# Retention into a Strassen-like feed-forward: layer-1 input sums on GpSimd, decays on the values

## The chip, the cores and the metric

The kernel runs on one core of one Trainium2 chip. Five engines of that core share the work, each with its own in-order queue of instructions: TensorE (PE in the profile, its weight loads as PEld), VectorE (DVE), ScalarE (ACT), GpSimd (POOL) and SyncE (SP), which here only issues DMAs. Engines wait for each other through semaphores; an instruction that waits holds up all that stands behind it on its own engine. The metric is the device time of one execution in microseconds, lower is better.

## The reference

All numbers are float32. The first part is a recurrent retention over 4 batches, 8 heads, 768 tokens and 64 features a head; the second is a feed-forward layer on the 3072 tokens that come out of it, with a gate that uses softplus and erf.

```python
gamma = 1.0 - 2.0 ** (-5.0 - np.arange(H))
for t in range(S):
    state = gamma * state + einsum('bhd,bhe->bhde', k[:, :, t], v[:, :, t])
    y[:, :, t] = scale * einsum('bhd,bhde->bhe', q[:, :, t], state)
x = y.transpose(0, 2, 1, 3).reshape(B * S, H * D)      # 3072 x 512
h = x @ w_in                                           # 512 -> 2048
sp = np.maximum(h, 0.0) + np.log1p(np.exp(-np.abs(h)))
out = (h * erf(sp)) @ w_out                            # 2048 -> 512
```

## The kernel before

**Retention by chunks.** The tokens are cut into 24 chunks of 128, numbered j; six of them make one batch. For a chunk the decays are folded into the inputs: a key is multiplied by its head's decay to the chunk's end, a query by the inverse, so that the scores are a plain product with a causal mask, and the state is a sum of products of scaled keys and values. Chunks 0 to 5 are scaled by `ret_scale` and transposed by TensorE. From chunk 6 on `prepared(j)` does it on VectorE alone, as a generator that its caller advances step by step: it scales the keys in token order (`KQ[j][:, 0]`, L579), which the state products read; it scales a second copy of the keys, `KB[j]`, and the queries, both loaded in 32x32 blocks (L588, twice); and it transposes those two by blocks (L592, twice). `sub_begin` and `sub_visit` then run the scores (L670), the state products `KQ` times `V` (L690, L814), the products of the masked scores with `V` (L793) and the products with the state (L778). The masked scores are written by `sub_mask` (L677).

**Loads.** `load(j)` issues 34 DMAs for a chunk from SyncE, in this order: the keys in token order (L208), 16 blocks of queries and 16 of keys (L190, 16 KB each), and last the values (`load_values`, L218). Each of these waits until the eighth DMA before it has landed. The calls are written into the order of the kernel by hand: chunks 6 and 7 are loaded during group 3, chunk j+3 after the visit of chunk j.

**Feed-forward.** The first 512 tokens (groups 0 to 3, each a quarter of the hidden features) are done with plain products, while weights are still converted and summed on VectorE (`sum_in`, L385). From group 4 (`G0`) on, 256 tokens take two groups, one for each half of the hidden features, and both layers use a scheme with 7 products in place of 8, the first layer nested so that 26 products of 128x128 tiles do. For these, `x_sums(g)` forms 18 sums or differences of 128x128 tiles of the layer's input, `xs`, before the first of the two groups (L969; the list is `X_SUMS`, in which a sum may use an earlier one). `xs` has one buffer, so its sums can only be written when the group before has read the old ones. `hidden_steps(g)` runs the 26 products in the order of `STEPS` (L987), each of which reads one sum or one input tile, and puts each into one of four PSUM banks, two named `hp` and two named `r`; it then adds the bank to the hidden blocks it belongs to (L999 on VectorE, L1001 and L1003 on ScalarE for the first of each block). The `r` banks are the ones that the scores use too.

**Order of a later group.** The 26 products, with parts of the second layer of the group before (`project_part`, L1070) between them; softplus on ScalarE (L859); the visit of a retention chunk; before an even group, `x_sums` of the next; on the others the preparation of a chunk; erf (L866); four more parts of the second layer; then the gate, two products on VectorE (`gated`, L885). In group 4 the order is written out apart: `prepared(6)`, `x_sums(4)`, the gate of group 3, the weight sums of the first half, the first step of `prepared(7)`, two weight sums, `sub_states(6)` (the mask and a state copy, L703), and then the 26 products.

**GpSimd** has almost no work: constants, small products of decay scales with 8 elements a partition (L496) or 32 (L522), and eight accumulating DMAs of 512 KB that form sums of the second layer's weights (`sums`, L394), each behind a negation on ScalarE (L393); the last of them stand in group 5.

Of the kernel before, what the change touches and what calls it, by code (L numbers as in the profile page):

```python
# [19 lines left out]
ALU = mybir.AluOpType  # L20
PSUM = bass.MemoryType.PSUM

P = 128
# [58 lines left out]
X_SUMS = (  # L82
    (0, (1, 0), (1, 1), "-"),
    (1, (0, 0), (0, 1), "-"),
    (2, (0, 0), (1, 0), "-"),
    (3, (1, 1), (0, 1), "-"),
    (4, (3, 0), (2, 0), "-"),
    (5, 1, 2, "-"),
    (6, (2, 0), 1, "+"),
    (7, (3, 1), 0, "-"),  # L90
# [39 lines left out]
)  # L130

OP = {"+": ALU.add, "-": ALU.subtract}

# [4 lines left out]
def kernel(  # L140
# [13 lines left out]
    nc = tc.nc  # L154
    B, H, S, D = q.shape
    d_model, d_ff = w_in.shape
    HP = H // 2
    NC = S // C
# [21 lines left out]
    KQ, V, KB = {}, {}, {}  # L180
# [39 lines left out]
    kq_s = const.tile([P, NC, 2, H], F32, name="kq_s")  # L220
# [268 lines left out]
    by = const.tile([P, H], F32, name="by")  # L489
# [13 lines left out]
    kq_b = const.tile([P, NC, 2, HP, 4], F32, name="kq_b")  # L503
# [71 lines left out]
    def prepared(j):  # L575

        if j >= NJ:
            return
        nc.vector.tensor_tensor(  # L579
            KQ[j][:, 0], KQ[j][:, 0],  # L580
            kq_s[:, j % NC, 0, :, None].to_broadcast([P, H, D]), op=ALU.mult,
        )
        yield
        blocks = (KB[j], KQ[j][:, 1].rearrange("p h d -> p (h d)"))
        for i, x in enumerate(blocks):
            x = x.rearrange("p (u a d) -> p u a d", u=HP, d=32)
            by = kq_b[:, j % NC, i, :, :, None].to_broadcast([P, HP, 4, 32])
            nc.vector.tensor_tensor(x, x, by, op=ALU.mult)  # L588
            yield
        for name, store, x in zip("kq", (KT, QT), blocks):  # L590
            store[j] = ret.tile([P, HP, C], F32, name=name + "T")
            nc.vector.transpose(store[j].rearrange("p u t -> p (u t)"), x)  # L592
            yield
# [354 lines left out]
    G0 = n_ft // FG  # L948
# [5 lines left out]
    def chunk_of(g):  # L954
        return TCH // SCH + (g - G0) // 2

    def x_sums(g):

        m = chunk_of(g)
        xs = ret.tile([P, N_X, P], F32, name="xs", bufs=1)  # L960

        def of(x):
            if isinstance(x, int):
                return xs[:, x]
            at = m % 2 * SCH + x[1] * P
            return XC[m // 2][:, x[0], at : at + P]

        for to, a, b, sign in X_SUMS:
            nc.vector.tensor_tensor(of(to), of(a), of(b), op=OP[sign])  # L969
        XS[m] = of  # L970

    def h_block(g, o):
# [251 lines left out]
    j = JPC + 2  # L1224
    sum_in(0, 20)
    all_of(prepared(j))
    x_sums(G0)
    load(j + 2)
    gated(G0 - 1)
# [3 lines left out]
    put_first(0)  # L1233
    sum_in(0, len(W_SUMS))
    next_chunk = prepared(j + 1)
    next(next_chunk)
    sum_in(1, 2)
# [28 lines left out]
    for g in range(G0 + 1, NG):  # L1266
# [4 lines left out]
        e_sums = g_sums(g - 1)  # L1271
        next(e_sums)
        next_chunk = prepared(j + 1) if even or put is None else iter(())

        if put is not None:
# [25 lines left out]
        if g + 1 < NG and not even:  # L1301
            x_sums(g + 1)
# [16 lines left out]
    g, m = NG - 1, chunk_of(NG - 1)  # L1319
# [10 lines left out]
    for i in range(2):  # L1330
# [4 lines left out]
        else:  # L1335
            last = ps_h.tile([P, TCH], F32, name="hp")[:, :P]
            a, b = PRODUCTS[3]
# [50 lines left out]
```

## Time and profile before

| | us |
|---|---|
| median of two runs | 661.3 |
| the two runs | 660.94, 661.66 |
| span of the profiled execution | 659.9 |
| a run's time beyond that span | 1.0 to 1.8 |
| TensorE busy | 654.1 |
| VectorE busy | 504.4 |
| ScalarE busy | 289.6 |
| GpSimd busy | 21.5 |

The profiled execution has no time of its own beside its span: what lies around the span is taken as the difference to the two runs, 1.4 us in the middle. The span is the time from the first to the last instruction. Busy times are sums over an engine's instructions; where an engine is busy for the whole of a stretch, only less work on it or a higher rate shortens that stretch. TensorE's ends are modelled, so its starts are the safer reading.

### The profile page before, as it was taken

The page shows a single profiled execution, that of the slowest core. Times are in us where ns is not written, and L with a number is a line of the kernel's source. Part 1 is how long each engine was busy: PE and PEld are TensorE (multiplying, and loading weights), DVE is VectorE, ACT ScalarE, POOL GpSimd, SP SyncE. Part 2 cuts the span into 40 slices and gives each one's busy share as a digit, 9 for nine tenths or more (in the row PEclk, how much of TensorE's full clock was granted, in tenths as well). Part 3 has the DMA queues.
Part 4 walks back from the last instruction along what each step waited for, and adds up shares of the span by engine and source line. Part 5 has one row for each costly group of instructions (what it writes and reads, how often), then busy time and mean ns, then how long its engine had stood idle before and what let it go on. Part 6 is the DMA issues. An engine that isn't in the chain of part 4 may idle for free.

```text
span 659.9 us, 15375 instructions
## 1 busy us (share of the span) xinstructions
PE 654.1 (99%) x6240; PEld 556.8 (84%) x6240; DVE 504.4 (76%) x1112; ACT 289.6 (44%) x410; POOL 21.5 (3%) x49
## 2 busy tenths in 40 slices
PE   8999999999999999999999999999999999999998
PEld 7744444487999999999999999999999999999997
DVE  5999879988886886787778678677787788476464
ACT  3468584527625334244254253342432542543440
POOL 1000061101100000000000000000000000000000
PEclk9999999999999999999999999999999999999999
DMA  9999972555843321222222322222231210000000
GB/s 190 222 236 220 211 246 43 107 100 120 165 77 59 79 47 35 68 44 48 68 46 45 73 39 50 60 52 42 38 80 34 45 55 1 1 35 1 1 32 33
DMA packets 157511, 51.90 MB, mean 79 GB/s; under 512 B 141312, under 2 KB 147840, under 8 KB 157440
## 3 DMA queue, kind: packets, MB, share of 16 engines
q1 hardware_dynamic: 155328, 46.71, 33.3%
q0 software_dynamic: 1696, 4.21, 3.4%
q8 instruction: 49, 0.80, 0.5%
q14 instruction: 22, 0.18, 0.1%
q10 hardware_dynamic: 416, 0.01, 0.0%
HBM read 40.39 MB, written 6.29 MB: 71 GB/s over the span
## 4 chain that ended last, share of the span: by engine, by line
PE 95%; DVE 3%; DMA 1%; SPq 0%; issue 0%; ACT 0%
PE o L1070 37%; PE hp L987 23%; PE r L987 12%; PE hp L896 8%; PE o L932 6%; PE r L778 2%; PE hp L670 1%; PE o L814 1%; DMA kq<-in_k_dram 1%; DVE w_in_sb L385 1%; PE r L599 1%; PE o L646 1%; PE r L793 1%; DVE xs L969 1%; PE hp L793 1%; PE r L566 1%
## 5 line engine op out<-in xcount | busy, mean ns | idle before, releaser
L987 PE MATMUL hp<-xs,w_in_sb 128*128 128x128 f32 x1040 | 145.6, 275 | 0.0
L1070 PE MATMUL o<-w_out_sb,h 128*128 128x256 f32 (+1 forms) x640 | 142.7, 380 | 0.0
L987 PEld LDWEIGHTS hp<-xs,w_in_sb 128*128 128x128 f32 x1040 | 135.2, 192 | 4.0 <-issue 0.7
L999 DVE TENSOR_TENSOR h<-h,hp 128x256 f32<-128x256 f32 x200 | 82.1, 419 | 73.6 <-PE hp L987 68.5
L1070 PEld LDWEIGHTS o<-w_out_sb,h 128*128 128x128 f32 x640 | 119.5, 190 | 16.6
L1070 PE MATMUL o<-w_out_sb,e 128*128 128x256 f32 x480 | 113.5, 379 | 0.0
L859 ACT ACTIVATE e<-h 128x2048 f32<-128x2048 f32 x22 | 42.0, 1910 | 120.6 <-DVE h L999 120.6
L1070 PEld LDWEIGHTS o<-w_out_sb,e 128*128 128x128 f32 x480 | 86.8, 190 | 9.4
L999 DVE TENSOR_TENSOR h<-h,r 128x256 f32<-128x256 f32 x160 | 59.9, 416 | 21.7 <-PE r L987 20.6
L1001 ACT COPY h<-hp 128x256 f32<-128x256 f32 x40 | 14.9, 373 | 134.6 <-PE hp L987 106.5
L987 PE MATMUL r<-xs,w_in_sb 128*128 128x128 f32 x480 | 66.7, 275 | 0.4 <-DVE am L677 0.4
L987 PEld LDWEIGHTS r<-xs,w_in_sb 128*128 128x128 f32 x480 | 60.0, 192 | 0.6 <-PE hp L987 0.6
L896 PE MATMUL hp<-xT,w_in_sb 128*128 128x512 f32 (+2 forms) x144 | 56.6, 548 | 0.0
L885 DVE TENSOR_TENSOR e<-h,e 128x1024 f32<-128x1024 f32 x42 | 49.3, 1213 | 8.0 <-ACT e L866 8.0
L987 PE MATMUL hp<-xT,w_in_sb 128*128 128x128 f32 x320 | 48.9, 275 | 0.0
L896 PEld LDWEIGHTS hp<-xT,w_in_sb 128*128 128x128 f32 x144 | 25.7, 190 | 27.2 <-issue 24.6
L987 PEld LDWEIGHTS hp<-xT,w_in_sb 128*128 128x128 f32 x320 | 43.6, 192 | 1.5 <-issue 0.5
L866 ACT ACTIVATE e<-e 128x2048 f32<-128x2048 f32 (+1 forms) x23 | 42.1, 1836 | 0.2
L1003 ACT ACTIVATE h<-hp 128x256 f32<-128x256 f32 x60 | 23.0, 384 | 31.1 <-PE hp L987 29.8
L987 PE MATMUL r<-xT,w_in_sb 128*128 128x128 f32 x240 | 33.3, 275 | 0.0
L866 ACT ACT_TABLE_LOAD x24 | 30.8, 1283 | 0.4
L987 PEld LDWEIGHTS r<-xT,w_in_sb 128*128 128x128 f32 x240 | 30.0, 192 | 0.0
(176 smaller groups left out, 778.6 us busy)
## 6 DMA issues: line engine op xcount, KB each, us to landing
w_out_sb<-in_moe_w_out_dram SPq DMA_DIRECT2D x14, 512.0 KB, 7.8
kq<-in_k_dram SPq DMA_DIRECT2D x23, 256.0 KB, 4.0
v<-in_v_dram SPq DMA_DIRECT2D x23, 256.0 KB, 3.4
out_dram<-r SPq DMA_DIRECT2D x23, 256.0 KB, 2.7
kq<-in_q_dram SPq DMA_DIRECT2D x288, 16.0 KB, 1.8
kb<-in_k_dram SPq DMA_DIRECT2D x288, 16.0 KB, 1.7
w_in_sb<-in_moe_w_in_dram SPq DMA_DIRECT2D x8, 512.0 KB, 13.2
w_out_sb<-w_out_sb POOLq DMA_DIRECT2D x8, 512.0 KB, 5.1
```

The costliest lines, as they stand in the source:

```text
L778: nc.tensor.matmul(pp[r][col * D : (col + 1) * D, u % 2, t], x[own, u, :], QT[j][own, u, t], start=first(r, col), stop=True, skip_group_ch ...
L793: nc.tensor.matmul(other[a][own, u % 2, D:] if crossed else pp[a][own, u % 2, t], V[j][t, 2 * u + r, :], AM[j][t, r, u, :D], start=crossed ...
L859: nc.scalar.activation(E[g], HS[g], AF.Softplus)
L866: nc.scalar.activation(E[g][:, half], E[g][:, half], AF.Erf)
L885: nc.vector.tensor_tensor(E[g][:, half], HS[g][:, half], E[g][:, half], op=ALU.mult)
L896: nc.tensor.matmul(HP_[ft][:, t], w_in_of(ft, kk), XC[0][:, kk, t], start=(kk == 0), stop=(kk == n_k - 1),)
L932: nc.tensor.matmul(O[0][tt].rearrange("p (d c) -> p d c", d=2), E[g][:, u * TCH + tt * P : u * TCH + (tt + 1) * P], w_out_of(ft), start=(f ...
L987: nc.tensor.matmul(to[:, u, :], w_in_sb[:, s, w, u * P : (u + 1) * P], XS[m](x), start=first and u == 0, stop=True, skip_group_check=True,)
L999: nc.vector.tensor_tensor(h, h, of, op=ALU.add if plus else ALU.subtract)
L1001: nc.scalar.copy(h, of)
L1003: nc.scalar.activation(h, of, AF.Copy, scale=-1.0)
L1070: nc.tensor.matmul(O[m][i][:, half, at], G[g][a][:, u * P : (u + 1) * P], w_out_sb[:, s, OUT[b], u, at], start=i not in started, stop=(s = ...
```

## The change

Two edits. In `prepared(j)`, from chunk 6 on, the values `V[j]` are multiplied by the decays of the keys, in place of the keys in both their copies; the queries are scaled as before. A score row weighted with scaled values, and the products for the state, come out the same, since each term holds one key and one value. Of the three products per chunk two remain; the place of the dropped one is kept as an empty step, so that the steps of the generator stand where they stood. In `x_sums` the 18 sums run on GpSimd for all but the first of the ten calls, and in all ten they follow a new order, `X_ORDER`; which sums there are, and of what, stays.

```diff
+X_ORDER = (1, 2, 5, 6, 9, 12, 13, 14, 0, 7, 15, 8, 4, 10, 11, 16, 17, 3)
 ...
         nc.vector.tensor_tensor(
-            KQ[j][:, 0], KQ[j][:, 0],
-            kq_s[:, j % NC, 0, :, None].to_broadcast([P, H, D]), op=ALU.mult,
+            V[j], V[j], kq_s[:, j % NC, 0, :, None].to_broadcast([P, H, D]), op=ALU.mult,
         )
         yield
+        yield
         blocks = (KB[j], KQ[j][:, 1].rearrange("p h d -> p (h d)"))
-        for i, x in enumerate(blocks):
-            x = x.rearrange("p (u a d) -> p u a d", u=HP, d=32)
-            by = kq_b[:, j % NC, i, :, :, None].to_broadcast([P, HP, 4, 32])
-            nc.vector.tensor_tensor(x, x, by, op=ALU.mult)
-            yield
+        x = blocks[1].rearrange("p (u a d) -> p u a d", u=HP, d=32)
+        by = kq_b[:, j % NC, 1, :, :, None].to_broadcast([P, HP, 4, 32])
+        nc.vector.tensor_tensor(x, x, by, op=ALU.mult)
+        yield
 ...
-        for to, a, b, sign in X_SUMS:
-            nc.vector.tensor_tensor(of(to), of(a), of(b), op=OP[sign])
+        engine = nc.vector if g == G0 else nc.gpsimd
+        for n in X_ORDER:
+            to, a, b, sign = X_SUMS[n]
+            engine.tensor_tensor(of(to), of(a), of(b), op=OP[sign])
```

## The prediction

> **What bounds the kernel now.** I read the page's busy times first, then the stages by group, then the timeline around the lines that change.
>
> ```profile
> PE 654.1 (99%) x6240; PEld 556.8 (84%) x6240; DVE 504.4 (76%) x1112; ACT 289.6 (44%) x410; POOL 21.5 (3%) x49
> ```
>
> ```profile
> 133.00:159.00 26.00, 25.59 (x238) 19.36 (x237) 22.83 (x59) 13.56 (x24) 1.74 (x2) 1.00 0.56 112
> 211.00:237.00 26.00, 26.00 (x291) 24.37 (x290) 20.00 (x52) 10.15 (x17) 0.00 (x0) 1.00 0.28 62
> ```
>
> The second view has two stages (length, then busy PE, PEld, DVE, ACT, POOL, then the granted clock). In a later group TensorE is busy for all of it at clock 1.00, and its products follow each other without a gap (eight 128x128 ones in 0.89 us, all along the chain). VectorE has some 6 us in 26 to spare. So work taken off VectorE shortens nothing by itself in groups 5 to 23, while a TensorE wait of any length moves the end by that length: no stretch behind it has idle time to take it back. The whole gain open to any such change is TensorE's idle time, 659.9 − 654.1 = 5.8 us. Faster by 2% (13.2 us), about what a measurement of this kernel can tell from no change, is all but excluded. The question is which waits are added. The matrix products are the same in number and order.
>
> **Part 1: values scaled in place of keys.** Eighteen chunks lose one 128x512 product of 0.68 us on VectorE. Nearly all of that time is idle cover in a bound TensorE stage: gain 0. The exception could be group 4:
>
> ```profile
> 131.32 0.69 PE L670 MATMUL r<-qT,kT 64*64 64x64 f32 x32
> ...
> 131.81 0.69 DVE L579 TENSOR_TENSOR kq<-kq,kq_s 128x512 f32<-128x512 f32 x1
> ...
> 132.53 0.47 SPq L218 DMA_DIRECT2D v<-in_v_dram  x1
> ...
> 133.08 0.75 DVE L677 TENSOR_TENSOR am<-r,causal_d 128x256 f32<-128x256 f32 x2
> ...
> 133.97 0.35 PE L987 MATMUL r<-xs,w_in_sb 128*128 128x128 f32 x1 [0.41 <-DVE am L677]
> ```
>
> The product at 131.81 is the first step of chunk 7's preparation. TensorE is late here: its third product of group 4 needs an `r` bank that the mask and the state copy on VectorE still read, and waits 0.4 us (against its usual distance, 133.39 to 133.97, 0.58). The dropped product of chunk 6 stood just ahead (its first step at 118.56), so VectorE would come 0.6 us earlier and this stall would go: −0.6 us if nothing else were late.
>
> But what is scaled now is the value tile, and it is the last of the chunk's 34 loads. The keys of chunk 7 were issued at 113.98; its values at 132.53, and they need 3.56 us:
>
> ```profile
> L218 SPq DMA_DIRECT2D v<-in_v_dram x1: 473/473/473, 132.5 to 132.5; - x1
> ...
> DMA to landing us min/median/max: 3.6/3.6/3.6
> ```
>
> So they land at 136.1, while VectorE asks for them at 131.8, or 131.2 with the dropped product. SyncE's pace in this stretch is set by landings of the small block loads (16 in 8.2 us, 16 in 9.7 us), which the change leaves alone. VectorE therefore stands still until 136.1, and behind the waiting product are two weight sums, the two masks and the state copy, which free the `r` bank. All of it slips by 136.1 − 131.8 = 4.3 us, and TensorE's product goes from 133.97 to 138.3. Behind that TensorE is bound to the end: **+4.3 us**, with the 0.6 us swallowed. Bounds: −0.6 if the values were there in time; +5.4 if they took 4.7 us, the slowest landing of the value loads behind them.
>
> For the other chunks I held each L218 landing (issue plus its landing time) against the L579 start: chunk 6 116.9 against 118.6, chunk 8 156.2 against 162.0, later ones 7 to 18 us early, with one close one, chunk 10 (203.56 against 203.70), in a group where VectorE has 2.5 us of idle time before the next product needs it. Cost there 0.
>
> **Part 2: sums on GpSimd.** Nine calls of 18 sums, 162 in all. On VectorE a sum starts every 0.20 us (0.28 long). Before, they end 1.5 us ahead of the first product that reads one. GpSimd's price is not in the trace, so I build it from its two-input rows:
>
> ```profile
> 5.33 0.21 POOL L496 TENSOR_TENSOR kq_s<-kq_s,by 128x8 f32<-128x8 f32 x1 [2.76 <-DVE kq_s L493]
> 5.63 0.73 DVE L556 TENSOR_TENSOR kq<-kq,kq_s 128x512 f32<-128x512 f32 x1
> 5.90 0.53 POOL L496 TENSOR_TENSOR kq_s<-kq_s,by 128x8 f32<-128x8 f32 x1
> ...
> 112.29 0.46 DVE L385 TENSOR_TENSOR w_in_sb<-w_in_sb 128x256 f32<-128x256 f32 x1
> 112.55 0.30 POOL L522 TENSOR_TENSOR kq_b<-kq_b,by_b 128x32 f32<-128x32 f32 x1
> ```
>
> Free, 8 elements take 0.21 us. Beside a VectorE product of two SBUF tensors the same takes 0.53 and ends 0.07 us after that product's end; with 32 elements, 0.10 after, and so do all five of that row. So the two engines exclude each other in such instructions, and what is left behind the lock grows by some 1.7 ns an element (0.04 us over 24). A free 128-element sum is then 0.21 + 120 × 1.7 ns = 0.41 us; one that waits for the sum before it starts 0.08 later (0.28 from start to start at 8 elements). Lower bound 0.29 (a one-input 128x128 selection, L459); upper 0.66, if the whole step from 0.21 to 0.30 over 24 elements is the rate. I take 0.41: a sum reads plain rows as the 8-element row does, the 32-element one reads a broadcast.
>
> By the Trainium skill's GPSIMD Engine Reference, section 3.1, a two-input add of 2048 elements takes 4497 ns; a line from the 8-element row to that gives an estimate of 0.46 us, and with it the sum below would be 0.4 us higher. No run here shows it yet.
>
> Now the race in a later group, with the profile's times:
>
> ```profile
> 229.08 0.56 DVE L834 TENSOR_TENSOR xT<-xT,hp 128x128 f32<-128x128 f32 x2 [0.44 <-ACT xT L832]
> ...
> 230.64 1.91 ACT L866 ACTIVATE e<-e 128x2048 f32<-128x2048 f32 x1
> ...
> 235.46 0.61 PE L987 MATMUL hp<-xs,w_in_sb 128*128 128x128 f32 x4
> ...
> 235.91 0.61 PE L987 MATMUL r<-xs,w_in_sb 128*128 128x128 f32 x4
> ```
>
> GpSimd can start at 229.45, 0.09 after the first of the two additions that complete the input. Seven sums, four of them waiting, are done by 232.56. The gate's two products (1.22 us each, two SBUF inputs) come when erf ends at 232.55, earlier than before since VectorE no longer has the sums; each holds GpSimd, with one sum between. The eighth sum (needed at 235.91) is done by 234.13, the ninth (236.35) by 235.6, the tenth (236.80) by 236.1, the fifteenth (239.48) by 238.3. Smallest margin 0.7 us: cost 0 in eight of nine calls. The same walk with 0.50 us a sum uses the margin up; with 0.66 the fifteenth comes 2.5 us late in every call.
>
> The first call, in group 5, differs: on GpSimd's queue stands the last accumulating DMA, which waits for its negation.
>
> ```profile
> 178.46 0.87 POOL L394 DMA_DIRECT2D w_out_sb<-w_out_sb  x1 [6.50 <-ACT w_out_sb L393]
> ```
>
> The sums start at 179.33, not 177.3. The gate comes at 181.5 after five sums, so the eighth is done at 184.99, while its product stands at 184.06: **+1.0 us** (0 without the lock, 4.2 at 0.66).
>
> **Sum.** 659.9 + 4.3 + 1.0 = 665.2 of span, plus the 1.4 us around it: **666.6 us**, 0.8% above the median of 661.3.
>
> **Rivals.**
> - *GpSimd too slow (slower).* From 0.50 us a sum on, each of the eight ordinary calls stalls TensorE; at 0.66 that is 8 × 2.5 + 4.2 + 4.3 = 28.5, so 690 us. For it: the 0.09 us step over 24 elements. Against: all 32-element products there ended behind a VectorE product, so that step is lock as much as rate. Over 2% needs about 1 us a call, some 0.57 us a sum. Chance 0.12; 0.05 more for small stalls (668 to 674).
> - *The value wait is not paid (no change).* If the values land before 131.2, the 0.6 us are won and only the first call costs: 661.7; without the lock 660.7. For it: the landings stand under two large accumulating DMAs whose timing may move. Against: the 5 us gap between issue order and need. Chance 0.11.
> - *The price falls elsewhere:* faster by over 2% would need work to leave TensorE; 0.01.
> - The forecast, 664 to 668.5: 0.71.
>
> By the Trainium skill's SBUF — State Buffer, section "Who interferes with whom", a VectorE instruction with only one SBUF input does not contend with GpSimd; the trace has no such pair. If the additions from PSUM (L999, from 237.5 on) contended too, the last needed sums would slip by 0.7 us, inside their 1.2 us of margin.
>
> Range 660.5 to 676: from the case without the value wait up to stalls of about 1.2 us in each ordinary call; it leaves out the slow end of the first rival. Faster 0.01, within 2% 0.87, slower 0.12.
>
> **What would show it.** After the change: VectorE idle some 4.5 us before the scaling of `v` at 131 to 136, released by a DMA of `in_v`; the first `r` product of group 4 waiting close to 5 us for `am`; GpSimd busy 70 to 90 us more, its sums 0.41 long when free and over 1 us under a gate; TensorE idle 1 us for `xs` in group 6 and not later. The prediction is wrong if group 4 runs as before, or if TensorE waits for GpSimd in every even group.

## The result and the profile after

The changed kernel takes **668.1 us** (668.08 to 668.11) against 661.3: a ratio of 1.0105, 95% interval 1.0088 to 1.0121. On the chip of a later experiment it took 668.3 against 661.1, ratio 1.0103 (1.0082 to 1.0125). The span of the profiled execution went from 659.9 to 666.4 us. The profiled execution of the kernel before is a rather long one of its kind: the median span of 29 later executions is 659.2, and of 21 others 659.4. One of the four executions of a later run, the one with the old order of the sums, took 845.5 us at a granted clock of 0.75 throughout and is left out. From the page after the change, busy time by engine:

```profile
PE 655.2 (98%) x6240; PEld 558.1 (84%) x6240; DVE 464.5 (70%) x932; ACT 289.9 (44%) x410; POOL 108.7 (16%) x211
```

VectorE lost 40 us of work, GpSimd took on 87, and TensorE, with the same 6240 products, sits idle for 11 us instead of 6. Line numbers are one to three higher than before in the places that matter. Two rows from the view of waits, for TensorE's products (total us, times, longest):

```profile
PE r L990 <- DVE am L678: 4.3, 1, 4.3
...
PE r L990 <- POOL xs L972: 0.9, 1, 0.9
```

From group 4 on these are the only two waits that are new in size: one for the mask in group 4, one for a sum on GpSimd. Both were forecast. The timeline of the first, start and length in us:

```profile
131.78 0.47 SPq L220 DMA_DIRECT2D v<-in_v_dram  x1
...
135.50 0.69 DVE L581 TENSOR_TENSOR v<-v,kq_s 128x512 f32<-128x512 f32 x1 [5.13 <-DMA v<-in_v_dram]
136.10 0.75 DVE L387 TENSOR_TENSOR w_in_sb<-w_in_sb 128x256 f32<-128x256 f32 x2
136.77 0.75 DVE L678 TENSOR_TENSOR am<-r,causal_d 128x256 f32<-128x256 f32 x2
...
137.67 1.66 PE L990 MATMUL r<-xs,w_in_sb 128*128 128x128 f32 x7 [4.34 <-DVE am L678]
```

Read it upwards: the third product waits for the masks, which stand behind two weight sums, which stand behind the scaling of the values, which waits 5.1 us for the last load of the chunk. The product starts at 137.67 instead of 133.97, 3.7 us later (3.9 when the 0.2 us that TensorE was ahead by then is counted).

The row counts seven instructions in 1.66 us. In the kernel before, eight at the same place took 1.13:

```profile
133.97 1.13 PE L987 MATMUL r<-xs,w_in_sb 128*128 128x128 f32 x8 [0.41 <-DVE am L677]
```

This is the part that the forecast did not have. The stretch in stages of 1 us; the columns are length, busy TensorE with its instructions, granted clock, DMA share and GB/s:

```profile
137.00:138.00 1.00, 0.33 (x2) 0.93 0.98 171
138.00:139.00 1.00, 1.00 (x7) 0.50 0.37 56
...
141.00:142.00 1.00, 1.00 (x10) 0.86 0.18 29
142.00:143.00 1.00, 1.00 (x11) 1.00 0.23 35
```

After the idle time TensorE's granted clock is halved for some 3.4 us (0.07 + 3 × 0.50 + 0.14 lost, doubled), and it does 6 or 7 instructions in a microsecond where it does 11 at full clock. It comes out 1.6 us further behind: 5.3 us in all when the clock is back. Of these, 0.2 come back at 143.7, where two products of the kernel before stood further apart. The wait in group 6 adds 1.0, and 0.2 more right behind it: the same 0.16 us stands there in all six profiled executions that have this wait, and in none of the four in which it is gone. Another 0.2 us of small delays was not followed up. 3.7 + 1.6 − 0.2 + 1.0 + 0.4 is the 6.5 us of the span.

### The profile page after: what moved, and what is told of

Its sections match the earlier page's. It is cut to its first block, busy times and chain, and to the rows that moved or that the text cites. A ratio compares the mean times of both kernels' runs of the same rounds, so it can differ in the third digit from the quotient of the medians.

```text
span 666.4 us, 15484 instructions
## 1 busy us (share of the span) xinstructions
PE 655.2 (98%) x6240; PEld 558.1 (84%) x6240; DVE 464.5 (70%) x932; ACT 289.9 (44%) x410; POOL 108.7 (16%) x211
## 4 chain that ended last, share of the span: by engine, by line
PE 89%; issue 7%; DMA 1%; POOL 1%; ACT 1%; DVE 0%; SPq 0%; POOLq 0%; ACTq 0%
PE o L1073 35%; PE hp L990 20%; PE r L990 11%; PE hp L897 8%; PE o L933 7%; PE r L779 1%; PE hp L671 1%; PE o L815 1%; POOL xs L972 1%; DMA kq<-in_k_dram 1%; DMA w_out_sb<-w_out_sb 1%; PE r L600 1%; PE o L647 1%; PE r L794 1%; PE r L568 1%
## 5 line engine op out<-in xcount | busy, mean ns | idle before, releaser
L990 PEld LDWEIGHTS hp<-xs,w_in_sb 128*128 128x128 f32 x1040 | 135.5, 192 | 3.9 <-issue 0.7
L972 POOL TENSOR_TENSOR xs<-xT 128x128 f32<-128x128 f32 x54 | 32.6, 623 | 331.7 <-DVE xT L835 331.7
L886 DVE TENSOR_TENSOR e<-h,e 128x1024 f32<-128x1024 f32 x42 | 52.8, 1297 | 35.4 <-ACT e L867 35.4
```

The source lines that it names most:

```text
L886: nc.vector.tensor_tensor(E[g][:, half], HS[g][:, half], E[g][:, half], op=ALU.mult)
L972: engine.tensor_tensor(of(to), of(a), of(b), op=OP[sign])
L990: nc.tensor.matmul(to[:, u, :], w_in_sb[:, s, w, u * P : (u + 1) * P], XS[m](x), start=first and u == 0, stop=True, skip_group_check=True,)
```

## The experiments

The explanation to test has three terms: the wait for the values (3.9 us net), the halved clock behind it (1.6 us), and the first call of the sums on GpSimd (1.0 us), with nothing for the other eight calls.

### One edit at a time

First the sums on GpSimd alone, with the keys scaled as before in `prepared`:

```diff
-            V[j], V[j], kq_s[:, j % NC, 0, :, None].to_broadcast([P, H, D]), op=ALU.mult,
+            KQ[j][:, 0], KQ[j][:, 0],
+            kq_s[:, j % NC, 0, :, None].to_broadcast([P, H, D]), op=ALU.mult,
...
+        for i, x in enumerate(blocks):        # KB[j] and the queries, as before
```

> The keys are scaled as before, in both copies; the sums stay on GpSimd in the new order. Theory: without a product that needs the values, the wait in group 4 goes, and with it the slow products behind it; only the first call of the sums still costs 1.0 us (and 0.3 us of small gaps): 662.3 to 662.6 us, GpSimd busy as in the changed kernel. Rival, the sums on GpSimd cost more than their one visible wait, by slowing VectorE's two-input products everywhere: 664 us or more.

Measured: 662.2 us against 660.9, ratio 1.0028 (1.0003 to 1.0053), 0.1 under the expected stretch. From group 4 on TensorE's only new wait is the one of 1.02 us from product to product in group 6, and the clock stays at 1.00 behind it. So the sums cost this one wait with the 0.2 us behind it, and their contention with VectorE costs nothing that shows. (The profiled execution took 666.0 us, since a weight load that landed late held up ScalarE, and with it TensorE, for 2.2 us at 87 us, with 3.4 us at half clock behind it; some executions of the kernel before reach 664 to 667 too.)

Then the scaled values alone:

```diff
-        engine = nc.vector if g == G0 else nc.gpsimd
+        engine = nc.vector
```

> The values are scaled as in the changed kernel; all ten calls of the sums run on VectorE, in the new order. Theory: the wait for the values (3.9 us more than the stall before) and the slow products behind it (1.6 us) stay, the 1.0 us in group 6 goes: 666.6 to 667.1 us. Rival, the sums on GpSimd share in the wait of group 4 (their DMAs or their lock): below 665.5 us.

Measured: 667.7 us, ratio 1.0086 (1.006 to 1.0112), 0.6 above the expected stretch. In its profiled execution the values landed later, at 136.6, the wait was 5.2 us, and the clock stayed at half for twice as long:

```profile
138.00:139.00 1.00, 0.21 (x1) 0.50 1.00 197
...
143.00:144.00 1.00, 1.00 (x6) 0.50 0.22 35
144.00:145.00 1.00, 1.00 (x8) 0.59 0.21 33
```

From 138.0 to 144.8 is 6.8 us, two of the earlier stretches. The halved clock is thus the term that varies: 1.6 us in one execution, 2.9 in another. The ten times of this kernel go from 666.5 to 669.5.

### The values first

```diff
         if j >= NB:
             KB[j] = loads.tile([P, HP * C], F32, name="kb", bufs=2)
-            nc.sync.dma_start(KQ[j][:, 0], k[b, :, now, :].rearrange("h p d -> p h d"))
+            load_values(j)
             load_blocks(KQ[j][:, 1].rearrange("p h d -> p (h d)"), q[b, :, now, :])
             load_blocks(KB[j], k[b, :, now, :])
...
+        if j >= NB:
+            nc.sync.dma_start(KQ[j][:, 0], k[b, :, now, :].rearrange("h p d -> p h d"))
-        if not early:
+        elif not early:
             load_values(j)
```

> From chunk 6 on the values are the first of a chunk's 34 loads and the keys in token order the last; all else as in the changed kernel. Theory: the values of chunk 7 land some 15 us before they are needed, TensorE's stall in group 4 falls from 4.5 us to 0 to 0.6 us, no product runs at half rate, the 1.0 us in group 6 stays: 661.3 to 662.3 us. Rival, VectorE is late there for another reason and the wait only changes its releaser: above 665 us.

Measured: 662.1 us against 660.9, ratio 1.0011 (0.9992 to 1.0031). The timeline around the place:

```profile
129.86 0.69 DVE L583 TENSOR_TENSOR v<-v,kq_s 128x512 f32<-128x512 f32 x1
...
132.52 0.76 DVE L680 TENSOR_TENSOR am<-r,causal_d 128x256 f32<-128x256 f32 x2 [1.31 <-PE r L693]
...
133.43 0.79 PE L992 MATMUL r<-xs,w_in_sb 128*128 128x128 f32 x5
```

The values are scaled at 129.9 without a wait; the mask is now the one that waits, for TensorE's state products (L693), and TensorE's third product follows at its usual distance, 0.55 us earlier than in the profiled execution of the kernel before. So the stall of that execution is gone too. The times do not show it as a gain: they lie 1.25 us above those of the kernel before, about as far as with the sums alone (1.3). Since its profiled execution was 0.7 us longer than its median, the stall may have been in that execution and not in most; there is no second trace of it. Two loads that swap places at the ends of the queue undo 6 us of the changed kernel's 668.1.

### Is it the idle time that halves the clock?

```diff
     for n, _ in enumerate(hidden_steps(G0), start=1):
+        if n == 2:
+            for _ in range(18):
+                nc.tensor.matmul(spare_bank, ident, ident, start=True, stop=True)
```

> The changed kernel, with 18 products of the identity with itself, some 4.0 us of TensorE work into a bank that nobody reads, put between the second and the third product of group 4, where TensorE waits for the values. Theory, the products behind the wait run at half rate because TensorE was idle: the wait stays, the granted clock is 1.00 all through, and the time falls by 1.6 us to 666.3 to 666.7. Rival, they run slow because of what they wait for (operands, banks) or the extra work costs what it saves: 668 us or more, products still 0.21 us apart.

Measured: 666.9 us, ratio 1.0089 (1.0055 to 1.0122); the expected 666.3 to 666.7 lies just below the median and well inside the spread of 666.1 to 667.8 that seven of the eight times have. The time alone decides little here. The trace does:

```profile
133.58 4.18 PE L1249 MATMUL o<-ident 128*128 128x128 f32 x36
136.75 0.69 DVE L581 TENSOR_TENSOR v<-v,kq_s 128x512 f32<-128x512 f32 x1 [4.91 <-DMA v<-in_v_dram]
138.93 1.13 PE L990 MATMUL r<-xs,w_in_sb 128*128 128x128 f32 x8 [1.17 <-DVE am L678]
```

```profile
140.00:141.00 1.00, 1.00 (x11) 1.00 0.14 23
```

(Each of the 18 products shows as two instructions.) VectorE waits 4.9 us for the values, which land 1.25 us later in this execution than in the changed kernel's, and the same third product starts late, at 138.93; but eight instructions behind it take 1.13 us and the clock is 1.00 throughout. Filled idle time, no slow products: the idle time is the cause, not what the products wait for.

### A shorter wait

```diff
-            load_blocks(KB[j], k[b, :, now, :])
+            load_blocks(KB[j], k[b, :, now, :], j)     # load_values(j) ahead of its last 4 blocks
```

> The changed kernel with a chunk's values issued 4 of its 16 key blocks sooner, so some 2.4 us. Theory: TensorE's stall in group 4 falls from 4.5 to about 2.1 us, which shows that the landing alone sets it. For the slow products behind it there are two cases: if any wait brings them in proportion, about 0.8 us of loss is left, 664.7; if only a wait of more than some length does, none is left and it comes to 663.9.

Measured once: 662.7 us. (In this and the other two runs that were measured once, the kernel before was also run once beside them and took 664.9, so that their times alone say little; the traces carry them.) The values were issued at 128.5 and landed at 131.9, 3.6 us earlier and not 2.4, so only 0.85 us of the stall is left and the case that I wanted, a wait of 2 us, did not come about. What it does show: 3.65 us less wait together with no slow product is 5.3 us, and the time fell by 5.4 from the changed kernel's 668.1.

### The first call of the sums

The group 6 race, in the changed kernel:

```profile
183.57 0.87 POOL L396 DMA_DIRECT2D w_out_sb<-w_out_sb  x1 [7.02 <-ACT w_out_sb L395]
184.14 1.20 POOL L972 TENSOR_TENSOR xs<-xT 128x128 f32<-128x128 f32 x2
...
186.53 1.37 DVE L886 TENSOR_TENSOR e<-h,e 128x1024 f32<-128x1024 f32 x1 [3.56 <-ACT e L867]
186.78 1.44 POOL L972 TENSOR_TENSOR xs<-xT,xs 128x128 f32<-128x128 f32 x1
...
188.29 1.31 POOL L972 TENSOR_TENSOR xs<-xT,xs 128x128 f32<-128x128 f32 x1
...
190.20 1.16 PE L990 MATMUL r<-xs,w_in_sb 128*128 128x128 f32 x8 [0.86 <-POOL xs L972]
```

Five sums, the gate, a sum stretched to 1.44, another to 1.31, and the eighth ends at 190.14, just ahead of the product that waited for it. The first two begin 0.57 us behind the start of the DMA and take 0.8 us each in place of 0.46, so that the third stands where it would if they had waited for the DMA's 0.87 us to end. The DMA ahead of them is the suspect for the late start:

```diff
+        if g + 1 < NG and not even:
+            x_sums(g + 1)
         if g == G0 + 1:
             all_of(last_steps)
-        if g + 1 < NG and not even:
-            x_sums(g + 1)
```

> The changed kernel with the last accumulating DMA behind the sums of group 6 on GpSimd's queue, not ahead of them. Theory: the sums start 0.1 us behind the chunk's last addition as in the other calls, and the wait of 1.0 us in group 6 is gone; the waits in group 4 stay: TensorE waits for no sum, about 667 us. Rival, the first call is late for another reason, such as a first use of the operation: the wait stays at 0.8 us or more.

Measured once: 667.9 us, and TensorE waits for no sum at all; the wait for `am` is unchanged at 4.3 us. The time fell by less than 1.0 only because the clock stayed at half for twice as long in this execution (2.9 us lost instead of 1.6). So the queue on GpSimd made the first call late.

### The order of the sums

```diff
-        for n in X_ORDER:
+        for n in range(N_X):
```

> The changed kernel with the 18 sums in their old order, 0 to 17, on GpSimd. Theory: sum 14, which the third product of each even group reads, is then the fifteenth and not the eighth. With 0.41 us from one sum to the next, 0.53 where it needs the one before, and the gate's two products holding GpSimd for 1.3 us each, it is ready 2.5 us late in the eight ordinary calls and 4.2 us in the first: 668 + 8 x 2.5 + 3.2 = 691 us, more if a wait of 2.5 us also brings slow products (1.6 us each, 704). Rival, the order does not matter because GpSimd is far enough ahead: 668.

Measured: 696.6, 697.7 and 701.3 us against 661.1, ratio 1.0557 (1.0523 to 1.0592). The order matters more than the engine, and by 6 us more than the waits that I had worked out. For the missing part another profile was taken:

> The old order of the sums on GpSimd again, for a profile at full clock. The three undisturbed times lay at 697 to 701 us, 6 to 10 above the 691 of the waits alone. Theory: the waits are 2.5 us in the ordinary calls and 4.2 us in the first, all for sum 14, and the rest is products 0.43 us apart in place of 0.22 behind some of them. Rival: the waits themselves are longer, 3.2 us or more, and the products behind them run at their usual distance.

Measured once: 694.6 us, with TensorE waiting 20.6 us for sums in nine places:

```profile
PE r L990 <- POOL xs L972: 20.6, 9, 3.6
```

From product to product, less the usual 0.11 us, the ordinary waits are 2.2 to 2.5 us and the first 3.7, a little under the forecast. What differs is what follows. The stages of 1 us behind two waits of the same length, in groups 10 and 14 (columns as above):

```profile
303.00:304.00 1.00, 0.77 (x6) 1.00 0.23 37
304.00:305.00 1.00, 1.00 (x11) 1.00 0.24 37
```

```profile
411.00:412.00 1.00, 0.65 (x3) 0.68 0.21 33
412.00:413.00 1.00, 1.00 (x6) 0.50 0.23 36
...
414.00:415.00 1.00, 1.00 (x8) 0.61 0.30 51
```

Behind a wait of 2.24 us (products at 300.88 and 303.23) the clock stays at 1.00; behind one of 2.24 us (409.00 and 411.35) it is halved for 3.4 us. Of the eight ordinary waits two were followed by slow products (1.6 us lost each, at 411 and 575), of the two long ones, the first call's and the one for the mask, both. The 26.5 us of span beyond the changed kernel's are 18.4 of ordinary waits, 2.7 more in the first call, 4.9 from three more stretches at half clock, and 0.5 of small delays. (The three earlier times stand at mean clocks of 0.985 to 0.987, against 0.990 here, which by estimate is one or two stretches more each; some 3 us of the 701.3 stay open.) The theory holds in kind, the count I did not foresee; the length of the wait does not settle it alone.

The traces show what does. The clock falls in this execution at 138.29, 192.90, 411.36 and 575.20 (worked out from stages such as the one at 411, whose mean of 0.68 puts the fall 0.36 us into it), and these times lie 16, 64 and 48 times 3.413 us apart. On that grid, two stretches behind which it stays and two behind which it falls, columns as above:

```profile
353.34:356.75 3.41, 1.76 (x13) 1.00 0.22 34
407.95:411.36 3.41, 1.34 (x12) 1.00 0.22 34
517.18:520.59 3.41, 1.84 (x13) 1.00 0.22 35
571.79:575.20 3.41, 1.40 (x11) 1.00 0.00 0
```

It is the busy time of TensorE within one such stretch that decides. In the twelve profiled executions at full clock, each divided on its own grid, the clock is halved behind every stretch with 1.41 us of busy TensorE or less, and stays behind every one with 1.76 or more. A halved clock came back behind stretches with 2.98 us or more, and stayed behind the two with 2.62 and 2.67: that is the difference between 3.4 and 6.8 us. A wait of 2.2 us costs its length alone where the grid divides it so that neither stretch comes that low. By the Trainium skill's TensorE: Matmul & The Clock Gate, section "What's actually happening", the clock is set from activity in windows of 3413 ns that run free, so that the outcome depends on where a wait lies among them. The grid agrees with that; the Trainium skill's page asks for a whole idle window, while here a window with 1.4 of its 3.4 us busy was enough, and the runs decide.

### Without the added waits

Two versions put the values first and leave no sum late: one has the sums of groups 4 and 6 on VectorE and the other eight calls on GpSimd, the other has all on VectorE.

```diff
-        engine = nc.vector if g == G0 else nc.gpsimd
+        engine = nc.vector if g <= G0 + 2 else nc.gpsimd     # the other version: nc.vector
```

> Values first and token-order keys last among a chunk's loads, and the sums of group 6 on VectorE too, so that GpSimd does the other eight calls. Theory: no added wait is left, and the stall of 0.6 us in group 4 goes with the dropped product: 0.5 to 0.7 us below the kernel before. Rival, the sums on GpSimd still cost by slowing VectorE's gate: the time of before or above.

> Values first and token-order keys last, all sums on VectorE in the new order. Theory: TensorE is bound in all groups from 5 on, so taking 162 sums off VectorE is worth nothing: the same time as with eight calls on GpSimd, 0.5 to 0.7 us below the kernel before. Rival, the freed VectorE time is worth something: above the run with eight calls on GpSimd by over 0.5 us.

Measured, against 661.1: 660.9 with eight calls on GpSimd, ratio 1.0001 (0.9986 to 1.0015), and 660.65 with none, ratio 0.9982 (0.9971 to 0.9994). The medians lie 0.2 and 0.4 us below the kernel before, the second's interval just clear of 1, and both gain less than the 0.5 to 0.7 us expected. In both profiles the stall in group 4 and all waits for sums are gone, and the span is 0.7 and 0.8 us shorter than the profiled one of before, 0.2 and 0.4 shorter than its median of 659.4. Between the two there is no gain from GpSimd to be seen: VectorE's freed time was not needed. The version with all sums on VectorE is the fastest of the study, 0.2% below the kernel before.

The changed kernel was run once more beside these:

> The changed kernel itself, on the chip of the next three. Theory: the wait for the values and the slow products behind it vary with the landing of one load, so 667 to 669 us, with the whole spread made before TensorE's third product of group 4 is some 20 products old; group 6 waits 1.0 us for a sum, no later group does.

Measured: 667.8 to 668.9 us, with the same two waits (4.5 and 1.0 us between products) and none in a later group. Its mean granted clock is 0.997 in two executions (both 667.8) and 0.995 in the other two (668.75 and 668.9), so that the spread follows the clock.

## Why the prediction was right, and where it was short

**The bound.** Right. TensorE is bound in every group from 5 on, waits there move the end one for one, and 30 us less on VectorE (468.4 against 498.9 busy in the last two versions) bought nothing. The intervals here reach 0.1 to 0.35% to each side, so a change of 1% is told apart from none, finer than the 2% that the forecast names.

**Part 1, the wait for the values.** Right in place, chain and size. Forecast: landing at 136.1, third product at 138.3, +4.3 us. Trace: ready at 135.5, product at 137.7, +3.9 us net; the load was issued 0.75 us earlier than in the profile before. Values first removes it. The 0.6 us put down to the dropped product appear at their place against the one profile of before, in versions without that wait; in the times 0.2 to 0.4 us at most are left of them.

**The step that was short** is the one behind it, "Behind that TensorE is bound to the end": it took the products after the wait at their usual price. They ran at half clock for 3.4 us, 1.6 us more (2.9 in some executions). The trace of before could have warned: its first products, the identity ones at the start, stand 0.21 us apart, twice as far as the same ones from 6.0 us on (0.11). That forecast and result lie only 1.5 us apart is in part luck: the wait moved the third product by 3.7 us and not 4.3, which took back 0.6 of the missing 1.6; the small delays less what came back add 0.2, and the time beyond the span 0.3 (1.7 us where 1.4 was taken). The result lies 0.4 us inside the stretch of 664 to 668.5 that got 0.71; two of the four later executions, 668.75 and 668.9, lie beyond it.

**Part 2, the sums.** A free sum was put at 0.41 us, 0.49 when it needs the one before; measured from start to start, 0.41 and 0.53. The line of an ordinary call, in the changed kernel:

```profile
239.08 1.31 DVE L886 TENSOR_TENSOR e<-h,e 128x1024 f32<-128x1024 f32 x1 [2.61 <-ACT e L867]
239.39 1.31 POOL L972 TENSOR_TENSOR xs<-xs 128x128 f32<-128x128 f32 x1
240.32 1.47 DVE L886 TENSOR_TENSOR e<-h,e 128x1024 f32<-128x1024 f32 x1
240.67 1.44 POOL L972 TENSOR_TENSOR xs<-xT 128x128 f32<-128x128 f32 x1
```

It is the forecast walk: sums, gate, one sum, gate, one sum, and the tenth done at 242.64, 0.7 us ahead of the product that reads it, as forecast (that product starts at 243.30). The two engines take turns: the sums beside the gate take 1.31 and 1.44 instead of 0.46, the gate's products 1.31 and 1.47 instead of 1.22. No ordinary call costs anything. The estimate of 0.46 us that the Trainium skill's GPSIMD Engine Reference, section 3.1, led to is the length that the trace shows; sums start closer together than that. The rule of the Trainium skill's SBUF — State Buffer, section "Who interferes with whom", on VectorE instructions with one SBUF input holds here: a sum at 243.97 beside an addition from PSUM at 244.01 takes 0.46 as when free.

**The first call.** Forecast 1.0 us, measured 1.02 and 0.16 behind it. Of its two causes the queue is shown by the run that moves the DMA behind the sums; the turns with the gate are read from the lengths of the sums (1.44 and 1.31 in place of 0.46, more than the whole wait) and have no run of their own.

**The rivals.** "GpSimd too slow" needed 0.50 us a sum and got 0.41; the run with the old order shows the same mechanism paid, through lateness and not through price. "The value wait is not paid" did not happen in any execution of the changed kernel.

## What to carry to other kernels

When a step is changed to read another tensor, look up where that tensor stands in its load queue: a value that used to be read last may be loaded last. On a bound TensorE an added wait costs its length and, from some 2 us on in these runs, can cost 1.6 to 2.9 us at half clock as well, so price both. Moving work off an engine that is not the bound bought nothing here, and on GpSimd what decided was the order of the results and what stands ahead in its queue.

## What was unexpected in the hardware

- TensorE's clock was halved for 3.4 us, or 6.8, behind all five waits of 4.5 us or more, behind one of 3.7 us, behind two of eight of 2.2 to 2.5 us, behind one of 2.2 us early in another kernel, and behind none of 1.3 us or less. What decided was TensorE's busy time in one stretch of a fixed grid of 3.413 us: halved at 1.41 us or less, not at 1.76 or more. Keeping TensorE busy with products that nobody reads prevented it.
- VectorE products of two SBUF tensors lose too when GpSimd reads beside them: 1.31 and 1.47 us instead of 1.22.
